# Narrow-tile matmuls of a pair of heads side by side, bank halves out of sequence, and GpSimd adds of half a tile

## The chip, the cores and the metric

The kernel runs on one core of one Trainium2 chip. The metric is the device time of one execution in microseconds. The engines of the core are TensorE (PE, with weight loads as PEld), VectorE (DVE), ScalarE (ACT), GpSimd (POOL) and SyncE (SP), which here issues nearly all DMAs. Each engine works through its own instructions in order and waits on semaphores for the others.

## The reference

Per head, attention over keys that fall in the same hash bucket; then a soft mixture of experts over all tokens.

```python
q, k, v: (4, 8, 768, 64) float32; proj: (64, 6)
q_bits, k_bits = (q @ proj > 0), (k @ proj > 0)          # 6 bits = 64 buckets
mask   = bucket(q)[:, :, :, None] == bucket(k)[:, :, None, :]
scores = where(mask, q @ k.T / 8, -1e9)
attn   = exp(scores - scores.max(-1)); attn /= attn.sum(-1) + 1e-9
x      = (attn @ v) as (3072, 512)                        # B*S tokens, H*D features
logits = x @ phi                                          # (3072, 32), 8 experts x 4 slots
d = softmax(logits, axis=0); slot_in = d.T @ x            # over tokens
slot_out[e] = relu(slot_in[e] @ w1[e]) @ w2[e]            # w1 512x1024, w2 1024x512
out = softmax(logits, axis=1) @ slot_out
```

## The kernel before

There are 32 heads (4 batches of 8), taken in pairs. A head has 768 queries and keys, as 6 blocks of 128. Per pair, `load` brings q and k, ScalarE and VectorE split them into high and low parts (`split_hi`, `split_lo`, tile w4), and SyncE moves the parts into the operand tiles XY of each head (`spread_y`, `spread_l`, `spread_x`, through `move`, L296). `bits` (L328) makes the hash bits of the pair with 32-column matmuls, and `spread_bits` moves them (tile bt) into XY. Three XY tiles go round.

Per head, `smax` (L370) multiplies for the row maxima: 12 matmuls, of 512 and 256 columns in turn, where matmuls n = 1 and 2 of every four fill two halves of one PSUM bank, behind which one VectorE reduction stands (L373; L376 for the whole banks). `shift` (L382 to L385) turns maxima into offsets, `shift_rows` (L404 transpose of 12 columns, L407 copy on ScalarE, a DMA mr into XY) puts them in a row of XY. `scores` (L421) then multiplies keys by queries, two matmuls each, in the same pattern of banks, and L425 takes the exponential into one of three tiles pt, each for two key blocks. `acc` adds the six key blocks of pt on GpSimd (L432 for the first two, L438 for the rest), 128x768 at a time. `av` (L449) multiplies by v for j = 0, 1, 2, each four matmuls with 64 columns of output on TensorE (the trace shows them as x8); v lies in one of two tiles, loaded by `load_v` (L278).

Per pair, `pair_sum` (L461) sums acc over keys with 32-column matmuls; L464 copies the sums on ScalarE, `pair_rec` takes reciprocals; `pair_log` (L476, 32 columns) makes the logits of the experts; `pair_turn` (L496) and `pair_x` (L511) transpose. After each eight heads a batch of the soft mixture is folded in (L607 to L661 and beyond); the experts' two layers and the output follow behind the last head, some 60 us. Their weights, 512 KB each, are loaded by `load_weights` (L190, L192) in between.

The order is written out by hand: `at` gives each piece a time, and a sort by it sets the order of the code. The times come from the table WHEN, in slots counted from the head's start (6 slots a head, even and odd heads apart), with overrides for the first and last heads in FIRST. Every engine's queue, SyncE's included, follows that order. SyncE's DMAs share eight semaphores in rotation.

Of the kernel before, what the change touches and what calls it, by code (L numbers as in the profile page):

```python
# [9 lines left out]
F32 = mybir.dt.float32  # L10
F32R = mybir.dt.float32r
AF = mybir.ActivationFunctionType
ALU = mybir.AluOpType
# [3 lines left out]
B, H, S, D, NB = 4, 8, 768, 64, 6  # L17
BH = B * H
P = 128
NT = S // P  # L20
HC = S // 2
# [12 lines left out]
N_Y = 3  # L34
# [7 lines left out]
C_ALL = C_FD + P  # L42


WHEN = {'load': -23.456,
 'bits': -14.465,
 'split_hi': -14.035,
 'split_lo': [-13.1, -12.626],
 'spread': [[-12.12, -11.747, -10.749, -7.5], [-12.05, -10.773, -10.639, -11.794]],
 'load_v': [-1.88, -1.85],  # L50
 'smax': [[-8.153, -7.646, -7.592, -7.407, -6.31, -6.263, -5.991, -5.086, -4.829, -4.442, -4.009, -3.019],
          [-7.926, -7.769, -7.645, -6.916, -6.247, -6.159, -6.133, -5.32, -4.829, -3.608, -3.608, -3.119]],
 'scores': [[-0.175, 0.609, 1.069, 1.557, 1.767, 2.599, 2.628, 3.37, 4.446, 4.862, 5.118, 5.577],
            [0.788, 1.398, 1.492, 1.906, 2.213, 2.62, 2.628, 3.37, 4.011, 4.193, 4.382, 4.945]],
 'shift': [-2.471, -2.398],
 'shift_rows': [-2.151, -1.917],
 'acc': [[5.646, 6.72, 8.258], [5.625, 6.02, 9.329]],
 'av': [[3.513, 6.554, 6.938], [3.513, 5.087, 6.68]],
 'pair_sum': 16.448,
 'pair_turn': 18.256,  # L60
 'pair_rec': [18.379, 18.389, 18.942],
 'pair_log': 18.557,
 'pair_x': [22.815, 24.33],
 'pair_add': 19.89,
 'batch_both': 20.1,
 'batch_max': 22.4,
 'batch_exp': 23.0,
 'batch_turn': 23.9,
 'batch_scale': 24.396,
 'batch_slots': 26.173,  # L70
 'batch_weigh': 24.65,
 'batch_share': 27.6,
 'load_weights': 4.18}

FIRST = {('load', 4): 4.476,
# [72 lines left out]
def lsh_attention_soft_moe(  # L148
# [11 lines left out]
    nc = tc.nc  # L160
# [35 lines left out]
    st = [dict() for _ in range(BH)]  # L196
# [8 lines left out]
    pts = [held.tile([P, 2 * S], F32, name=f"pt{j}") for j, held in enumerate((ap, lp, mp))]  # L205
    accs = [(mp if i == (BH - 1) % 3 else ap).tile([P, S], F32, name=f"acc{i}") for i in range(3)]
    vs = [held.tile([P, NT, D], F32, name=f"v{i}") for i, held in enumerate((ap, mp))]
# [31 lines left out]
    p_sm = ps_stack.enter_context(tc.tile_pool(name="p_sm", bufs=2, space=PSUM))  # L239
    p_st = ps_stack.enter_context(tc.tile_pool(name="p_st", bufs=3, space=PSUM))  # L240
# [13 lines left out]
    Ys, Xs = [], []  # L254
    XYs = []
    for i in range(N_Y):
        held = lp if i == (BH - 1) % N_Y else yp
        XYs.append(held.tile([P, 2, 2, S], F32R, name=f"XY{i}"))
        Xs.append(XYs[i][:, :, 0])
        Ys.append(XYs[i][:, :, 1])  # L260
    row = accs[0][0:1]
    nc.gpsimd.memset(row, 1.0)

# [10 lines left out]
    lacc_of = {}  # L274

    def load_v(h):
        st[h]["v"] = vs[h % 2]
        nc.sync.dma_start(out=st[h]["v"], in_=vt[h])  # L278


# [13 lines left out]
    def move(dst, src, eng=nc.sync):  # L294

        eng.dma_start(out=dst.bitcast(F32), in_=src.bitcast(F32))  # L296


    def spread_y(h):
        s = st[h]  # L300
        s["XY"], s["Y"] = XYs[h % N_Y], Ys[h % N_Y]
        if h == 0:
            return
        r = 64 * (h % 2)
        move(s["Y"][0:64], s["w4"][r:r + 64, 0::2])
# [6 lines left out]

    def spread_x(h):
        s = st[h]
        s["X"] = Xs[h % N_Y]
        r = 64 * (h % 2)
        move(s["X"][0:64], s["w4"][r:r + 64, 0::3])
        move(s["X"][96:128], s["w4"][r + 32:r + 64, 1:3])
# [40 lines left out]

    def smax(h, t, part):  # L360
        s = st[h]
        if t == 0 and part == 0:
            s["mx"] = mp.tile([P, NT, 2], F32, name="mx", bufs=2)
        mx = s["mx"].rearrange("p t a -> p (t a)")
        n = 2 * t + part
        if n % 4 != 2:
            s["sm_ps"] = p_sm.tile([P, 512], F32, name="smx")
        pt = s["sm_ps"]
        o, a, b = ((0, 0, 512), (0, 512, S), (256, 0, 256), (0, 256, S))[n % 4]
        nc.tensor.matmul(pt[:, o:o + b - a], s["Y"][0:96, 0, t * P:(t + 1) * P], s["Y"][0:96, 1, a:b],  # L370
                         start=True, stop=True)
        if n % 4 == 2:
            nc.vector.tensor_reduce(out=mx[:, n - 1:n + 1], in_=pt.rearrange("p (a x) -> p a x", a=2),  # L373
                                    axis=AX.X, op=ALU.max)
        elif n % 4 != 1:
            nc.vector.reduce_max(out=mx[:, n:n + 1], in_=pt, axis=AX.X)  # L376
# [34 lines left out]
    def scores(h, i, part):  # L411
        s = st[h]
        n = 2 * i + part
        if n % 4 == 0:
            s["P", i // 2] = pts[i // 2]
        if n % 4 != 2:
            s["st_ps"] = p_st.tile([P, 512], F32, name="st")
        pt = s["st_ps"]
        o, a, b = ((0, 0, 512), (0, 512, S), (256, 0, 256), (0, 256, S))[n % 4]
        for x, first in ((s["Y"], True), (s["X"], False)):  # L420
            nc.tensor.matmul(pt[:, o:o + b - a], x[:, 1, i * P:(i + 1) * P], x[:, 0, a:b],  # L421
                             start=first, stop=not first)
        if n % 4 != 1:
            u = (0, 0, 1, 2)[n % 4]
            nc.scalar.activation(s["P", i // 2][:, 512 * u:512 * u + 512], pt, AF.Exp, scale=D ** -0.5)  # L425

    def acc(h, j):
        s = st[h]
        pr = s["P", j]
        if j == 0:  # L430
            s["acc"] = accs[h % 3]
            nc.gpsimd.tensor_tensor(out=s["acc"], in0=pr[:, 0:S], in1=pr[:, S:2 * S], op=ALU.add)  # L432
        else:
            for a in range(2):
                n = 2 * j + a
                eng = nc.vector if h == BH - 1 and n > 2 else nc.gpsimd
                if h < BH - 1 or n < NT - 1:
                    eng.tensor_tensor(out=s["acc"], in0=s["acc"], in1=pr[:, a * S:(a + 1) * S], op=ALU.add)  # L438

    def av(h, j, half=None):  # L440
        s = st[h]
# [273 lines left out]
    def at(when, f, *args):  # L715
        key = (f.__name__, *(a for a in args if isinstance(a, int)))
        plan.append((FIRST.get(key, when), len(plan), (f, *args)))
# [10 lines left out]
    for h in range(BH):  # L728
        s0, x = NT * h, h % 2
        if x == 0:  # L730
            if h > 0:
                at(s0 + WHEN["load"], load, h)
            at(s0 + WHEN["bits"], bits, h)
            at(s0 + WHEN["split_hi"], split_hi, h)
            for n in range(2):
                at(s0 + WHEN["split_lo"][n], split_lo, h, n)
        for n, f in enumerate((spread_y, spread_bits, spread_l, spread_x)):
            at(s0 + WHEN["spread"][x][n], f, h)
        at(s0 + WHEN["load_v"][x], load_v, h)
        for n in range(2 * NT):  # L740
            at(s0 + WHEN["smax"][x][n], smax, h, n // 2, n % 2)
            at(s0 + WHEN["scores"][x][n], scores, h, n // 2, n % 2)
        at(s0 + WHEN["shift"][x], shift, h)
        at(s0 + WHEN["shift_rows"][x], shift_rows, h)
        for j in range(NT // 2):
            lone = h == BH - 1 and j == NT // 2 - 1
            at(s0 + (5.725 if lone else WHEN["acc"][x][j]), acc, h, j)
            if lone:
                for n in range(2):
                    at(s0 + 5.85 + n, av, h, j, n)  # L750
            else:
                at(s0 + WHEN["av"][x][j], av, h, j)
        if x and h < BH - 1:
            p, p0 = h - 1, s0 - NT
            at(p0 + WHEN["pair_sum"], pair_sum, p)
            at(p0 + WHEN["pair_turn"], pair_turn, p)
            for n in range(3):
                at(p0 + WHEN["pair_rec"][n], pair_rec, p, n)
            at(p0 + WHEN["pair_log"], pair_log, p)
            at(p0 + WHEN["pair_x"][0], pair_x, p, (0, 1))  # L760
            at(p0 + WHEN["pair_x"][1], pair_x, p, (2,))
            at(p0 + WHEN["pair_add"], pair_add, p)
        if h % H == H - 1 and h < BH - 1:
            for f in (batch_both, batch_max, batch_exp, batch_turn, batch_scale, batch_slots, batch_weigh, batch_share):
                at(p0 + WHEN[f.__name__], f, h // H)
    last, h = NT * BH, BH - 1
# [62 lines left out]
    for x in range(2):  # L829
        pt = p_mi.tile([P, 512], F32, name="mi")[:, 0:2 * P]  # L830
# [179 lines left out]
```

## Time and profile before

| | |
|---|---|
| three runs, us | 521.5, 524.3, 527.04 (median 524.3) |
| the profiled execution's own time, us | 524.46 |
| its span, us | 522.4 |
| mean granted clock of TensorE | 0.987 |
| busy: PE, DVE, ACT, POOL, us | 499.2, 369.3, 246.6, 326.8 |
| chain that ended last, by engine | PE 70%, DVE 10%, DMA and its queue 13%, POOL 2% |

A row of the timeline gives start and length in us, the engine, the line, the operation, what it writes and reads, the form, and a count where equal instructions are joined; in brackets the idle time before it and what ended it. Matmuls overlap, so the price of one is the distance from its start to the next start, not its length. A row of the groups gives total busy time and mean ns. A row of the chain is a piece of the path that ended last. A row of the windows gives busy time of the engines in one stretch, then the clock, the share of DMA time and the rate.

### The profile page before, as it was taken

Reading aid. Unit: us, or ns where it says so; the run is one execution under the profiler, and the core shown is the slowest. Engines: PE = TensorE matmul, PEld = TensorE weight load, DVE = VectorE, ACT = ScalarE, POOL = GpSimd, SP = SyncE. Lnnn points to the kernel's source line nnn. Section 1 sums busy time; section 2 is a strip of 40 time slices with the busy share of each in tenths; the row PEclk is TensorE's granted clock in tenths of the full one; section 3 lists DMA queues with packets and bytes.
Section 4 is the critical chain, followed back from the end, with each engine's and each line's share of the span. In section 5 each row is a group of like instructions: output and inputs, shape, how many; then the busy total and the mean of one; then the engine's idle time right before and its main releaser. Section 6 shows DMA issues by size and latency. Waiting matters only on the chain.

```text
span 522.4 us, 9095 instructions
## 1 busy us (share of the span) xinstructions
PE 499.2 (96%) x3164; PEld 284.3 (54%) x3164; DVE 369.3 (71%) x703; ACT 246.6 (47%) x463; POOL 326.8 (63%) x223
## 2 busy tenths in 40 slices
PE   7968999999999999999999999999999999999992
PEld 4544555555555555556554555565555555553562
DVE  6574877787878787777787788787777885464233
ACT  4144536464646454545454545454644545422232
POOL 9246767676739776767488785856588767411200
PEclk9789999999999999999999999999999999999998
DMA  5747475758585657575765757676636366879967
GB/s 126 188 98 188 116 196 173 193 168 197 169 197 168 178 143 203 152 210 143 217 149 167 183 175 178 188 181 182 146 101 154 73 156 234 319 286 352 410 275 293
DMA packets 39777, 99.59 MB, mean 191 GB/s; under 512 B 7458, under 2 KB 13732, under 8 KB 39732
## 3 DMA queue, kind: packets, MB, share of 16 engines
q1 hardware_dynamic: 39540, 98.94, 66.3%
q8 instruction: 25, 0.41, 0.3%
q14 instruction: 20, 0.16, 0.1%
q0 software_dynamic: 192, 0.08, 0.1%
HBM read 52.76 MB, written 6.29 MB: 113 GB/s over the span
## 4 chain that ended last, share of the span: by engine, by line
PE 70%; DVE 10%; SPq 7%; DMA 6%; POOL 2%; issue 2%; ACT 1%; DVEq 0%; ACTq 0%; POOLq 0%
PE st L421 20%; PE av L449 19%; PE smx L370 13%; SPq L296 7%; DMA XY<-bt 4%; PE qs L933 3%; DVE w L292 3%; PE qh L851 3%; DVE mx L376 3%; PE mi L461 2%; PE mi L476 2%; POOL acc L438 1%; PE mi L328 1%; DMA w<-w 1%; DMA XY<-w 1%
## 5 line engine op out<-in xcount | busy, mean ns | idle before, releaser
L438 POOL TENSOR_TENSOR acc<-acc,pt 128x768 f32<-128x768 f32 x125 | 238.8, 1911 | 39.4 <-ACT pt L425 27.1
L425 ACT ACTIVATE pt<-st 128x512 f32<-128x512 f32 x288 | 162.0, 595 | 97.2 <-PE st L421 90.8
L421 PE MATMUL st<-XY 128*128 128x512 f32 (+1 forms) x768 | 183.7, 347 | 0.0
L376 DVE TENSOR_REDUCE mx<-smx 128x1 f32<-128x512 f32 x192 | 130.8, 687 | 54.1 <-PE smx L370 53.8
L449 PE MATMUL av<-pt,v 128*64 128x384 f32 x768 | 145.3, 499 | 0.0
L370 PE MATMUL smx<-XY 96*128 96x512 f32 (+1 forms) x384 | 126.6, 375 | 9.9 <-DVE mx L376 5.4
L421 PEld LDWEIGHTS st<-XY 128*128 128x128 f32 x768 | 123.7, 191 | 21.1 <-issue 10.6
L370 PEld LDWEIGHTS smx<-XY 96*128 96x128 f32 x384 | 70.1, 191 | 74.4 <-DVE mx L376 26.1
L432 POOL TENSOR_TENSOR acc<-pt 128x768 f32<-128x768 f32 x32 | 58.6, 1830 | 63.8 <-ACT pt L425 63.8
L449 PEld LDWEIGHTS av<-pt,v 128*64 128x64 f32 x768 | 46.5, 136 | 62.7 <-issue 57.5
L373 DVE TENSOR_REDUCE mx<-smx 128x2 f32<-128x512 f32 x96 | 65.6, 683 | 4.3 <-PE smx L370 4.1
L292 DVE TENSOR_TENSOR w<-raw,w 128x768 fp32r<-128x768 f32 x30 | 41.2, 1373 | 3.7 <-ACT w L288 3.7
L468 DVE RECIPROCAL sm<-sm 128x128 f32<-128x128 f32 x45 | 39.6, 910 | 0.0
L288 ACT CAST w<-raw 128x768 fp32r<-128x768 f32 x32 | 25.1, 831 | 19.5 <-DMA XY<-w 9.7
L453 ACT COPY avs<-av 128x384 f32<-128x384 f32 x32 | 15.3, 478 | 37.2 <-PE av L449 37.2
L407 ACT CAST mr<-mi 12x128 fp32r<-12x128 f32 x31 | 7.9, 255 | 49.2 <-PE mi L404 44.6
L321 DVE TENSOR_SCALAR bt<-mi,con 128x384 fp32r<-128x384 f32 x15 | 10.1, 677 | 25.3 <-DMA XY<-bt 9.6
L607 POOL TENSOR_TENSOR dl<-lacc,dl 64x384 f32<-64x384 f32 x3 | 3.0, 999 | 25.6 <-ACT dl L606 25.6
L513 DVE TENSOR_TENSOR xq<-mi,r 128x256 f32<-128x256 f32 x45 | 17.3, 412 | 0.4 <-PE mi L511 0.4
L328 PE MATMUL mi<-raw,pb 128*32 128x384 f32 x128 | 15.2, 517 | 0.1
L933 PE MATMUL qs<-w 128*32 128x256 f32 x232 | 15.2, 382 | 0.0
L511 PE MATMUL mi<-ident,avs 128*128 128x128 f32 x90 | 14.8, 273 | 0.0
(173 smaller groups left out, 339.4 us busy)
## 6 DMA issues: line engine op xcount, KB each, us to landing
w<-w SPq DMA_DIRECT2D x61, 512.0 KB
XY<-w SPq DMA_DIRECT2D x63, 384.0 KB
raw<-qk SPq DMA_DIRECT2D x32, 384.0 KB
XY<-w SPq DMA_DIRECT2D x64, 192.0 KB
v<-vt SPq DMA_DIRECT2D x32, 192.0 KB
out<-w SPq DMA_DIRECT2D x12, 512.0 KB
xq<-w SPq DMA_DIRECT2D x3, 512.0 KB
XY<-bt SPq DMA_DIRECT2D x62, 19.5 KB
```

The lines of the kernel that those rows point to most:

```text
L292: (nc.vector if h else nc.gpsimd).tensor_tensor(out=w[:, 2 * x + 1], in0=st[h]["raw"][:, x], in1=w[:, 2 * x], op=ALU.subtract)
L296: eng.dma_start(out=dst.bitcast(F32), in_=src.bitcast(F32))
L370: nc.tensor.matmul(pt[:, o:o + b - a], s["Y"][0:96, 0, t * P:(t + 1) * P], s["Y"][0:96, 1, a:b], start=True, stop=True)
L373: nc.vector.tensor_reduce(out=mx[:, n - 1:n + 1], in_=pt.rearrange("p (a x) -> p a x", a=2), axis=AX.X, op=ALU.max)
L376: nc.vector.reduce_max(out=mx[:, n:n + 1], in_=pt, axis=AX.X)
L421: nc.tensor.matmul(pt[:, o:o + b - a], x[:, 1, i * P:(i + 1) * P], x[:, 0, a:b], start=first, stop=not first)
L425: nc.scalar.activation(s["P", i // 2][:, 512 * u:512 * u + 512], pt, AF.Exp, scale=D ** -0.5)
L432: nc.gpsimd.tensor_tensor(out=s["acc"], in0=pr[:, 0:S], in1=pr[:, S:2 * S], op=ALU.add)
L438: eng.tensor_tensor(out=s["acc"], in0=s["acc"], in1=pr[:, a * S:(a + 1) * S], op=ALU.add)
L449: nc.tensor.matmul(s["av"][64 * c:64 * c + 64, 0:HC], s["v"][:, i, :], pr[:, o + c * HC:o + (c + 1) * HC], start=(i == 0), stop=(i == NT - 1))
L468: nc.vector.reciprocal(out=rs[:, k * P:(k + 1) * P], in_=rs[:, k * P:(k + 1) * P])
L933: nc.tensor.matmul(po[32 * j:32 * j + 32], hTs[g][:, f, 32 * j:32 * j + 32], wt[1, x, 2 * g + f // 4, j][:, (f % 4) * HM:(f % 4 + 1) * HM] ...
```

## The change

The table of times is new in nearly all entries, and code is changed so that the new order can be built: the two halves of a bank may be issued apart, with other banks between them, and the tiles of a head are known from the start. GpSimd adds 384 columns at a time, twice as often. The last head keeps its old times for av. The numbers of instructions are else unchanged.

```diff
-WHEN = {'load': -23.456,
+WHEN = {'load': -20.249,
...
- 'load_v': [-1.88, -1.85],
+ 'load_v': [-0.013, 1.668],
...
+    for h in range(BH):
+        st[h].update(XY=XYs[h % N_Y], X=Xs[h % N_Y], Y=Ys[h % N_Y], v=vs[h % 2], acc=accs[h % 3])
+        st[h].update((("P", j), pt) for j, pt in enumerate(pts))
...
     def smax(h, t, part):
         s = st[h]
-        if t == 0 and part == 0:
+        if "mx" not in s:
             s["mx"] = mp.tile([P, NT, 2], F32, name="mx", bufs=2)
...
         if n % 4 != 2:
-            s["sm_ps"] = p_sm.tile([P, 512], F32, name="smx")
-        pt = s["sm_ps"]
+            s["sm_ps", n] = p_sm.tile([P, 512], F32, name="smx")
+        pt = s["sm_ps", n - (n % 4 == 2)]
...
     def scores(h, i, part):
...
-            s["st_ps"] = p_st.tile([P, 512], F32, name="st")
-        pt = s["st_ps"]
+            s["st_ps", n] = p_st.tile([P, 512], F32, name="st")
+        pt = s["st_ps", n - (n % 4 == 2)]
...
         if j == 0:
-            s["acc"] = accs[h % 3]
-            nc.gpsimd.tensor_tensor(out=s["acc"], in0=pr[:, 0:S], in1=pr[:, S:2 * S], op=ALU.add)
+            for c in (slice(0, HC), slice(HC, S)):
+                nc.gpsimd.tensor_tensor(out=s["acc"][:, c], in0=pr[:, 0:S][:, c], in1=pr[:, S:2 * S][:, c], op=ALU.add)
...
                 if h < BH - 1 or n < NT - 1:
-                    eng.tensor_tensor(out=s["acc"], in0=s["acc"], in1=pr[:, a * S:(a + 1) * S], op=ALU.add)
+                    for c in (slice(0, HC), slice(HC, S)):
+                        eng.tensor_tensor(out=s["acc"][:, c], in0=s["acc"][:, c], in1=pr[:, a * S:(a + 1) * S][:, c], op=ALU.add)
...
-                at(s0 + WHEN["av"][x][j], av, h, j)
+                at(s0 + (WHEN["av"][x][j] if h < BH - 1 else (3.513, 5.087)[j]), av, h, j)
```

Line numbers move up by one or two from L278 on (av is L448, the sums L460, the logits L475, the XY moves L298), v's load is L280.

The first place is TensorE in a pair of the middle of the run, around the sums. pt_81 to pt_83 are the three tiles of exponentials, v_87 and v_88 the v of the even and the odd head, XY_133 to XY_135 the operands of three heads, acc_85 and acc_86 the sums over key blocks. Before:

```order
L449 MATMUL av<-pt_81,v_87 64x384 x4
L370 MATMUL smx<-XY_135 128x512
L404 MATMUL mi<-ident,mz 12x128
L370 MATMUL smx<-XY_135 128x256 x2
L421 MATMUL st<-XY_133 128x512 x2
L461 MATMUL mi<-acc_85,ones 32x384 x2
L461 MATMUL mi<-acc_86,ones 32x384 x2
L370 MATMUL smx<-XY_135 128x512
```

and in the changed kernel:

```order
L448 MATMUL av<-pt_81,v_87 64x384 x4
L460 MATMUL mi<-acc_85,ones 32x384 x2
L460 MATMUL mi<-acc_86,ones 32x384 x2
L404 MATMUL mi<-ident,mz 12x128
L370 MATMUL smx<-XY_135 128x512
L419 MATMUL st<-XY_133 128x256 x2
```

The sums and the transpose of the odd head's offsets now follow directly on the even head's first product with v. Some rows on, on TensorE, around the logits, before:

```order
L496 MATMUL mi<-ident,sm 128x128 x3
L449 MATMUL av<-pt_82,v_87 64x384 x4
L476 MATMUL mi<-avs,phs 32x384 x4
L421 MATMUL st<-XY_134 128x512 x2
L370 MATMUL smx<-XY_135 128x512
L449 MATMUL av<-pt_83,v_87 64x384 x4
L370 MATMUL smx<-XY_135 128x512
```

and in the changed kernel:

```order
L370 MATMUL smx<-XY_135 128x512
L475 MATMUL mi<-avs,phs 32x384 x4
L448 MATMUL av<-pt_82,v_87 64x384 x4
L448 MATMUL av<-pt_83,v_87 64x384 x4
L370 MATMUL smx<-XY_135 128x512 x2
L419 MATMUL st<-XY_134 128x512 x4
```

The logits now stand ahead of the second and third product of the even head, which are side by side.

The second place is SyncE's queue of the same pair from the row move (mr) of the odd head on; w_2724 and w_2816 are the split parts (w4), w is a weight of the experts. Before:

```order
L296 DMA XY_134<-mr 1x12x128
L278 DMA v_88<-vt 128x384
L190 DMA w<-w 128x1024
L296 DMA XY_135<-w_2724 64x2x768
L296 DMA XY_135<-w_2724 32x2x768
L296 DMA XY_133<-w_2724 64x2x768 x2
L296 DMA XY_133<-w_2724 32x2x768
L296 DMA XY_133<-bt 13x384 x2
L296 DMA XY_133<-bt 12x384 x2
```

and in the changed kernel:

```order
L298 DMA XY_134<-mr 1x12x128
L190 DMA w<-w 128x1024
L298 DMA XY_135<-w_2816 64x2x768
L298 DMA XY_135<-w_2816 32x2x768 x2
L298 DMA XY_133<-w_2816 64x2x768
L298 DMA XY_133<-bt 13x384 x2
L298 DMA XY_133<-bt 12x384 x2
L280 DMA v_88<-vt 128x384
```

The load of the odd head's v went from the second place to the last, and one large move of XY_133 to behind it.

The third place is SyncE's queue at the last two heads, where the experts' weights are loaded. Before:

```order
L278 DMA v_87<-vt 128x384
L190 DMA w<-w 128x1024 x4
L296 DMA XY_134<-mr 1x12x128
L278 DMA v_88<-vt 128x384
L190 DMA w<-w 128x1024 x4
L192 DMA w<-w 128x1024 x11
```

and in the changed kernel:

```order
L280 DMA v_87<-vt 128x384
L190 DMA w<-w 128x1024 x3
L298 DMA XY_134<-mr 1x12x128
L190 DMA w<-w 128x1024 x4
L192 DMA w<-w 128x1024 x2
L280 DMA v_88<-vt 128x384
L192 DMA w<-w 128x1024 x9
```

The last head's v now stands behind six weight loads.

More of the change, by code (lines that the diff above doesn't have):

```diff
@@ L42 @@
 C_ALL = C_FD + P
-WHEN = {'load': -23.456,
[L46 to L49, printed above, removed]
- 'load_v': [-1.88, -1.85],
[L51 to L72, printed above, removed]
+WHEN = {'load': -20.249,
+ 'bits': -14.229,
+ 'split_hi': -14.469,
+ 'split_lo': [-12.593, -12.307],
+ 'spread': [[-8.873, -8.628, -4.884, -6.051], [-10.66, -10.364, -10.117, -8.499]],
+ 'load_v': [-0.013, 1.668],
+ 'smax': [[-7.891, -7.253, -6.89, -6.827, -4.575, -5.887, -4.897, -4.184, -4.405, -3.626, -3.436, -6.587],
+          [-8.119, -7.886, -7.155, -6.373, -6.078, -6.011, -4.493, -5.588, -3.625, -2.796, -2.553, -3.994]],
+ 'scores': [[-0.043, 1.163, 1.625, 2.761, 0.577, 1.651, 2.152, 4.632, 5.195, 4.559, 5.142, 4.685],
+            [-0.586, -0.207, 1.227, 2.283, 2.074, -0.029, 2.493, 3.261, 5.447, 3.307, 5.002, 5.509]],
+ 'shift': [-2.838, -2.089],
+ 'shift_rows': [-2.486, -1.921],
+ 'acc': [[3.889, 5.034, 5.737], [3.898, 5.254, 6.706]],
+ 'av': [[3.899, 7.565, 7.571], [3.365, 5.792, 6.373]],
+ 'pair_sum': 15.998,
+ 'pair_turn': 17.461,
+ 'pair_rec': [17.523, 18.844, 17.946],
+ 'pair_log': 19.428,
+ 'pair_x': [18.368, 24.222],
+ 'pair_add': 19.51,
+ 'batch_both': 19.679,
+ 'batch_max': 21.206,
+ 'batch_exp': 23.21,
+ 'batch_turn': 25.393,
+ 'batch_scale': 25.508,
+ 'batch_slots': 27.498,
+ 'batch_weigh': 27.829,
+ 'batch_share': 29.729,
  'load_weights': 4.18}
@@ L276, in load_v @@
     def load_v(h):
-        st[h]["v"] = vs[h % 2]
         nc.sync.dma_start(out=st[h]["v"], in_=vt[h])
@@ L300, in spread_y @@
         s = st[h]
-        s["XY"], s["Y"] = XYs[h % N_Y], Ys[h % N_Y]
         if h == 0:
@@ L314, in spread_x @@
         s = st[h]
-        s["X"] = Xs[h % N_Y]
         r = 64 * (h % 2)
@@ L413, in scores @@
         n = 2 * i + part
-        if n % 4 == 0:
-            s["P", i // 2] = pts[i // 2]
         if n % 4 != 2:
-            s["st_ps"] = p_st.tile([P, 512], F32, name="st")
-        pt = s["st_ps"]
+            s["st_ps", n] = p_st.tile([P, 512], F32, name="st")
+        pt = s["st_ps", n - (n % 4 == 2)]
         o, a, b = ((0, 0, 512), (0, 512, S), (256, 0, 256), (0, 256, S))[n % 4]
```

## The prediction

> **What bounds the kernel now.** I read the split of busy time first, then the chain that ended last, then the timeline of TensorE over one pair of heads, then the DMA issues of SyncE over the same pair. The first row gives stretch, its length, and the busy time of PE, PEld, DVE, ACT and POOL, the granted clock, DMA share and GB/s:
>
> ```profile
> 60.00:380.00 320.00, 317.79 (x1871) 180.60 (x1869) 251.01 (x454) 166.84 (x312) 227.16 (x127) 1.00 0.66 176
> ```
>
> TensorE is without work for 2.2 of 320 us at clock 1.00, while GpSimd has 93 us free and VectorE 69. So in the attention part the time is what TensorE's queue costs, one instruction after another. The chain gives the length of a pair. Its rows are start, length, engine and work; each av row below with 8 matmuls is the first product with v of an even head:
>
> ```profile
> 60.56 1.44 PE av L449 x8
> ...
> 223.04 1.44 PE av L449 x8
> ...
> 246.87 0.92 PE st L421 x4
> 249.21 1.44 PE av L449 x8
> ...
> 278.42 1.44 PE av L449 x8
> ...
> 357.59 1.44 PE av L449 x8
> ```
>
> From 223.04 to 249.21 a pair takes 26.17 us. From 249.21 to 278.42 it takes 29.21, because that pair holds a batch of the soft MoE (L661). The eleven pairs from 60.56 to 357.59 take 297.03; two of them hold a batch, so the other nine take (297.03 - 2 x 29.21) / 9 = 26.51. That is 0.34 above the clean 26.17: what a pair loses on average to waits. The row at 246.87 gives the plain price of a 512-column matmul: 0.92 / 4 = 0.23.
>
> Where the 26.17 holds something other than plain matmuls shows in the timeline (start, length, line, form):
>
> ```profile
> 197.54 0.50 PE L370 MATMUL smx<-XY 96*128 96x512 f32 x1
> 197.88 0.27 PE L404 MATMUL mi<-ident,mz 128*12 128x128 f32 x1
> 197.91 0.48 PE L370 MATMUL smx<-XY 96*128 96x256 f32 x2
> 198.23 0.63 PE L421 MATMUL st<-XY 128*128 128x512 f32 x2
> 198.79 0.85 PE L461 MATMUL mi<-acc,ones 128*32 128x384 f32 x8
> 199.57 0.50 PE L370 MATMUL smx<-XY 96*128 96x512 f32 x1
> 199.91 1.10 PE L421 MATMUL st<-XY 128*128 128x256 f32 x6
> ...
> 201.74 1.51 PE L449 MATMUL av<-pt,v 128*64 128x384 f32 x8
> 203.18 0.85 PE L476 MATMUL mi<-avs,phs 64*32 64x384 f32 x8
> ```
>
> and, from the last head,
>
> ```profile
> 458.05 0.87 PE L449 MATMUL av<-pt,v 128*64 128x384 f32 x4
> 458.84 0.44 PE L511 MATMUL mi<-ident,avs 128*128 128x128 f32 x2
> ```
>
> The reader is to compare starts. Two 512-column matmuls ahead of the sums take 198.79 - 198.23 = 0.56, which is 0.09 more than 2 x 0.233: the price of going into narrow tiles (64 or 32 columns). The 512-column matmul behind them takes 199.91 - 199.57 = 0.34, so 0.105 more: the price of coming back. Half an av group takes 458.84 - 458.05 = 0.79, so two halves apart would be 1.58, against 203.18 - 201.74 = 1.44 for a whole one: 0.14 is paid inside a group once per visit. A visit of av thus costs 0.09 + 0.14 + 0.105 = 0.33 beyond its work. The lone L404 pays as well: the matmul ahead of it takes 0.34, the two 256-column ones behind it 0.32 in place of 0.24.
>
> **The change part by part.** *Neighbours on TensorE.* Before, a pair visits narrow tiles at av, L404, L461, av with L476, av, av with L328 and L404, av, av. After, the order has av with sums and L404; logits and two av; av with L404 and bits; av; av. Eight visits become five. (a) The sums beside av: gone are one return behind av (0.105), the return behind the lone L404 (0.10), and the entry ahead of the sums (0.09), together 0.30. The change between 64 and 32 columns is not free: av takes 1.44 ahead of L476, as ahead of a full matmul, so I count that exit in full on both sides. (b) The logits and two av in a row: one return (0.105), one entry (0.09) and one inside price (0.14), together 0.33. (c) L404 ahead of bits in place of behind: 0. The sum is 0.63 a pair, or 15 x 0.63 = 9.5 us. (d) The batch's matmuls (L661) also stand beside av: one entry and one return, 0.2 to 0.3, in three batches: 0.7 us. The Trainium skill, page "TensorEngine Tiling (Array Packing)", Key Properties, states that changing the tiling mode, and not just the tile, drains TensorE; 1.44 ahead of L476 agrees. Taken alone the rule would count changes, 18 a pair before and 13 after, which at half a visit (0.165) each is 0.8 a pair and 12.4 us in all.
>
> *Bank halves out of sequence.* The matmuls, exponentials and maxima are as many as before, so 0 on TensorE. A bank is now held from its first half to the second, while others pass; three st banks and two smx banks bear that in the order, except that about 0.1 us of waiting for a maximum is possible at some places. Before, waits cost 0.34 a pair by the above; the bits now come earlier in front of the maxima that need them. I take those 0.34 down to 0.13, so -3 (from -5 with all gone to +3 with 0.2 more).
>
> *GpSimd by halves.* These are two rows of the groups (mean ns behind the comma), and below them three of the chain:
>
> ```profile
> L438 POOL TENSOR_TENSOR acc<-acc,pt 128x768 f32<-128x768 f32 x125 | 238.8, 1911 | 39.4 <-ACT pt L425 27.1
> L607 POOL TENSOR_TENSOR dl<-lacc,dl 64x384 f32<-64x384 f32 x3 | 3.0, 999 | 25.6 <-ACT dl L606 25.6
> ```
>
> ```profile
> 127.14 2.37 DMA XY<-bt
> 132.27 0.86 DVE w L292
> 133.74 2.42 DVE w L292
> ```
>
> A half is bounded by 1911 / 2 = 0.96 from below and by the 384-column add's 1.00, with some 0.08 between two, from above. Ten adds a pair then take 19.1 to 21.6 us in place of 19.1, in a pair of 25.5. That stays off the path: the cover is some 4 us of GpSimd's own slack, so 0. VectorE's w (L292) takes 0.86 alone and up to 2.42 when it meets GpSimd; with halves it can be held about 1.0 less at a time, which is part of the -3 above. The Trainium skill, page "SBUF — State Buffer", Who interferes with whom, states that such a VectorE instruction with two SBUF inputs contends with a GpSimd instruction that reads SBUF; 0.86 against 2.42 agrees.
>
> *v of the odd head.* In SyncE's queue this load moves from right behind the row move (mr) to behind one weight load, four moves of w and the four of bt. SyncE's rows of that burst before, the DMA of the same stretch (last two figures: share, GB/s), and the sizes of these loads:
>
> ```profile
> 225.39 0.78 SPq L296 DMA_DIRECT2D XY<-mr  x1
> 226.21 0.50 SPq L278 DMA_DIRECT2D v<-vt  x1
> 226.75 0.43 SPq L190 DMA_DIRECT2D w<-w  x1
> 227.23 6.05 SPq L296 DMA_DIRECT2D XY<-w  x5
> 233.33 4.25 SPq L296 DMA_DIRECT2D XY<-bt  x4
> ```
>
> ```profile
> 225.40:238.30 12.90, 12.90 (x84) 6.86 (x82) 10.02 (x19) 6.20 (x11) 8.48 (x6) 1.00 0.74 184
> ```
>
> ```profile
> w<-w SPq DMA_DIRECT2D x61, 512.0 KB
> XY<-w SPq DMA_DIRECT2D x63, 384.0 KB
> ...
> XY<-w SPq DMA_DIRECT2D x64, 192.0 KB
> v<-vt SPq DMA_DIRECT2D x32, 192.0 KB
> ```
>
> I add up the new order with the prices above (the clean pair of before comes to 26.15 in this way, against 26.17 measured). In pair time, 0 being the first av of the even head, L404 of the odd head then stands at 2.2, and its row move issues some 1.0 later, since the logarithm of the sums (L464 before) now goes ahead of the copy on ScalarE: 3.2. The odd head's first av stands at 14.05. Early bound: without backlog an XY move issues in about 0.7 and a bt move in 0.75, so v issues at 0.8 + 0.43 + 4 x 0.7 + 4 x 0.75 = 7.0 after mr, takes 0.5, and lands 2.4 later (the 2.37 of the bt move): 9.9, so 13.1 of the pair, 0.9 in time. Late bound: with the backlog shown, w, XY and bt took from 226.75 to 237.58 = 10.8; with one XY fewer 9.6; then 0.8 + 9.6 + 0.5 + 2.4 = 13.3, so 16.5, or 2.4 late. By bytes: 2.3 MB (0.5 of w, 1.5 of three large and two small XY moves, 0.2 of v, the rest small) went in 12.9 us at 184 GB/s; now one large XY move less, 1.9 MB, go, v last, in 10.5 plus about 1 of landing. I take the middle of the bounds, 11.6, which the bytes support: v lands at 14.8 and TensorE stands 0.75. Behind av on its queue then waits everything else, so it is paid in full. The weight load is there for 12 odd heads; the other three are 0.5 MB / 184 = 2.8 earlier and in time. So +9.0 us, from 0 to 29.
>
> *v of the last head.* It now stands behind six weight loads of 512 KB; before it was ahead of them. SyncE's rows, the DMA while the loads run, and TensorE's first av of heads 30 and 31:
>
> ```profile
> 441.32 0.69 SPq L278 DMA_DIRECT2D v<-vt  x1
> 442.58 1.75 SPq L190 DMA_DIRECT2D w<-w  x4
> ```
>
> ```profile
> 442.58:453.20 10.62, 10.62 (x63) 4.46 (x61) 4.20 (x7) 5.37 (x11) 7.78 (x5) 1.00 0.85 315
> ```
>
> ```profile
> 438.44 1.51 PE L449 MATMUL av<-pt,v 128*64 128x384 f32 x8
> ...
> 451.40 1.51 PE L449 MATMUL av<-pt,v 128*64 128x384 f32 x8
> ```
>
> Its first av ran 451.40 - 438.44 = 12.96 behind that of head 30. The loads can start once head 30's last scores are done, 5.4 behind head 30's first av in the new order; 3.3 MB at 315 GB/s take 10.6, and a landing lags about 1: 17 against 13.1. I take 3.6 (from 0, were v to overtake the loads, to 5). All that follows shifts with it.
>
> *Start and the MoE's end:* same work, 0.
>
> The sum: -9.5 - 0.7 - 3 + 9.0 + 3.6 = -0.6, and +2 for waits of the new order on maxima and row moves that I can't place (the row move lands 0.1 us ahead of its scores, bounds -1 and +5): +1.4. Against the profiled run's own 524.46 that is 526. The median of the runs is 524.3, so it stands equal.
>
> **The rivals.** A: v of odd heads is in time, since SyncE's queue is freer than in the burst shown. For it: the early bound, 0.9 to spare. Against: the bytes. Then 526 - 9 = 517, and 513 if the last v is also in time. B, the other side: the backlog holds as shown, v is 1.3 to 2.4 late, the late bound. It decides from a landing 12.2 us after mr on; the price is 12 x 1.8 = 22 in place of 9: 539. C: narrow neighbours save less than thought, as each change of columns pays what a visit paid: only two av in a row gain, 0.33 a pair, 526 + 4.5 = 530. Against it: the entry and return are seen on the full matmuls around, which are fewer. D: GpSimd's halves cost over 1.27 each, so twenty exceed the pair of 25.5; at 1.35 a pair is 27: 526 - 9 (v is then in time) + 12 x 1.5 = 535. Against it: the 1.00 of L607.
>
> **How the numbers follow.** My forecast, v late by 0.2 to 1.2 a pair, 519 to 532, gets 0.47; A 0.27; B 0.14; C 0.08; D 0.04. About 1% (519.2 to 529.7) is what a measurement can tell from no change. Faster: 0.25 of A and 0.03 of mine, 0.28. Slower: B, D, half of C and 0.11 of mine, 0.33. Within 1%: 0.39. The range 515 to 538 leaves out the fast edge of A (0.08) and the slow half of B with D's edge (0.1).
>
> **What would show it.** A pair without waits of 25.5 in the chain; sums starting 1.44 behind the even head's first av; the second of two av groups at 1.29; GpSimd's half at 0.96 to 1.04. TensorE's waits should name v's load at the odd head's first av, about 0.75 each in 12 pairs, and once 3 to 4 us at head 31. No such wait and a pair of 25.6 would prove A; waits of 2 us B; pairs of 26 without waits C. If TensorE waits chiefly for maxima or row moves, the step that put waits at -3 and +2 was wrong.

## The result and the profile after

The changed kernel takes 545.5 us (median of four runs, 541.38 to 550.04), against 523.65 for the kernel before beside it: a ratio of 1.0385, with a 95% interval of 1.0294 to 1.0475. The forecast was 526, with 515 to 538 as its range. The profiled execution of the changed kernel has a span of 543.7 us. All ratios, here and below, are taken over executions in the faster of the chip's two states and against executions of the kernel before from the same round, while the times are medians of all executions, so a difference of two times from different rounds can be off by one or two us.

The same window as before the change, the middle of the attention part (busy time of PE, PEld, DVE, ACT, POOL, clock, DMA share, GB/s):

```profile
60.00:380.00 320.00, 302.82 (x1787) 179.04 (x1787) 249.73 (x432) 154.81 (x294) 229.16 (x236) 1.00 0.64 167
```

TensorE now stands 17 of 320 us, where it stood 2; VectorE and GpSimd are about as busy as they were although fewer heads pass in the window, ScalarE is less so for that reason, and the clock is the same. So the loss is waiting. The list of TensorE's waits (us in total, times, longest) names what for:

```profile
PE av L448 <- DMA v<-vt: 15.6, 14, 1.5
PE mi L404 <- DVE mz L385: 5.2, 16, 0.6
PE smx L370 <- DVE mx L376: 4.5, 3, 3.8
PE st L419 <- ACT pt L423: 1.6, 3, 0.8
```

The third row is nearly all at the start, as before. The first is new; the second stood there once before, with 1.1 us. The list counts only idle time behind the modelled end of a matmul. A lone 512-column matmul is 0.40 long in the rows while the next one starts 0.23 behind it, so a delay of some 0.1 us shows in the starts alone. TensorE's timeline shows where in a pair the waits fall; here are the rows that matter of the pair from 230.12 to 257.76:

```profile
230.12 1.51 PE L448 MATMUL av<-pt,v 128*64 128x384 f32 x8
231.56 0.85 PE L460 MATMUL mi<-acc,ones 128*32 128x384 f32 x8
232.69 0.28 PE L404 MATMUL mi<-ident,mz 128*12 128x128 f32 x1 [0.28 <-DVE mz L385]
232.90 0.47 PE L370 MATMUL smx<-XY 96*128 96x512 f32 x1
...
238.40 0.85 PE L475 MATMUL mi<-avs,phs 64*32 64x384 f32 x8
239.18 2.80 PE L448 MATMUL av<-pt,v 128*64 128x384 f32 x16
241.91 0.73 PE L370 MATMUL smx<-XY 96*128 96x512 f32 x2
...
245.69 1.51 PE L448 MATMUL av<-pt,v 128*64 128x384 f32 x8 [0.86 <-DMA v<-vt]
247.14 0.28 PE L404 MATMUL mi<-ident,mz 128*12 128x128 f32 x1
247.34 0.85 PE L328 MATMUL mi<-raw,pb 128*32 128x384 f32 x8
...
257.76 1.51 PE L448 MATMUL av<-pt,v 128*64 128x384 f32 x8
```

The pair takes 27.64 where the order summed to 25.5. The neighbours themselves cost what was forecast: the sums follow 1.44 behind av, the logits take 0.78, and the two av in a row take 2.73 to the next start, which is 1.44 + 1.29. But L404 starts 2.57 into the pair, not 2.2; the odd head's first av starts 15.57 into it, not 14.05. I took the starts of every pair against the plain prices. Over the ten pairs without a batch that hold bits, from 59 to 430 us, the medians are: L404 0.37 late, and the next matmul 0.21 behind it where 0.03 was usual (0.55 in all); 0.17 more behind the second L404, ahead of bits; 1.2 at that av; and 0.35 in pieces, most of them of 0.07 to 0.1 and ahead of scores. With the 25.5 that makes 27.8, against a median pair of 27.9. From the first even head's first av to the last one's the changed kernel needs 423.1 us, against 404.7; the start is 0.5 shorter, and what follows 3.5 longer.

### The profile page after: what moved, and what is told of

It reads as the page before. It is cut to its first block, busy times and chain, and to the rows that moved or that the text cites. A ratio compares the mean times of both kernels' runs of the same rounds, so it can differ in the third digit from the quotient of the medians.

```text
span 543.7 us, 9273 instructions
## 1 busy us (share of the span) xinstructions
PE 501.1 (92%) x3164; PEld 293.1 (54%) x3164; DVE 384.6 (71%) x705; ACT 242.9 (45%) x463; POOL 340.1 (63%) x380
## 4 chain that ended last, share of the span: by engine, by line
PE 55%; DVE 15%; DMA 12%; SPq 12%; issue 3%; ACT 2%; DVEq 0%; ACTq 0%
PE st L419 16%; PE av L448 12%; SPq L298 11%; PE smx L370 10%; DMA v<-vt 8%; DVE mx L376 4%; DVE mx L373 4%; DVE mz L385 3%; PE qs L932 3%; PE qh L850 3%; DVE mz L383 2%; PE mi L328 2%; DMA XY<-mr 2%; PE mi L510 2%; PE mi L475 2%
## 5 line engine op out<-in xcount | busy, mean ns | idle before, releaser
L437 POOL TENSOR_TENSOR acc<-acc,pt 128x384 f32<-128x384 f32 x250 | 249.2, 1027 | 41.7 <-ACT pt L423 41.7
L419 PE MATMUL st<-XY 128*128 128x512 f32 (+1 forms) x768 | 176.2, 344 | 1.7 <-ACT pt L423 1.6
L448 PE MATMUL av<-pt,v 128*64 128x384 f32 x768 | 143.1, 500 | 16.9 <-DMA v<-vt 15.6
L376 DVE TENSOR_REDUCE mx<-smx 128x1 f32<-128x512 f32 x192 | 128.9, 685 | 35.4 <-PE smx L370 35.2
L370 PE MATMUL smx<-XY 96*128 96x512 f32 (+1 forms) x384 | 132.5, 381 | 6.1 <-DVE mx L376 4.5
L419 PEld LDWEIGHTS st<-XY 128*128 128x128 f32 x768 | 126.8, 190 | 19.5 <-ACT pt L423 5.9
L430 POOL TENSOR_TENSOR acc<-pt 128x384 f32<-128x384 f32 x64 | 62.6, 999 | 74.6 <-ACT pt L423 74.3
L448 PEld LDWEIGHTS av<-pt,v 128*64 128x64 f32 x768 | 49.4, 137 | 82.7 <-issue 64.3
L290 ACT CAST w<-raw 128x768 fp32r<-128x768 f32 x32 | 25.1, 830 | 29.9 <-DMA XY<-mr 22.4
L294 DVE TENSOR_TENSOR w<-raw,w 128x768 fp32r<-128x768 f32 x30 | 29.8, 994 | 9.9 <-ACT w L290 9.9
L385 DVE SCALAR_TENSOR_TENSOR mz<-m,mz 128x6 f32<-128x6 f32 x32 | 28.6, 893 | 1.1
L463 ACT ACTIVATE sm<-mi,eps 128x384 f32<-128x384 f32 x15 | 8.7, 581 | 24.7 <-PE mi L460 24.7
L512 DVE TENSOR_TENSOR xq<-mi,r 128x256 f32<-128x256 f32 x45 | 16.6, 395 | 0.4 <-PE mi L510 0.3
L404 PEld LDWEIGHTS mi<-ident,mz 128*12 128x12 f32 x31 | 2.6, 85 | 26.1 <-DVE mz L385 15.3
L383 DVE TENSOR_SCALAR mz<-m 128x6 f32<-128x6 f32 x32 | 15.2, 474 | 1.1
## 6 DMA issues: line engine op xcount, KB each, us to landing
XY<-bt SPq DMA_DIRECT2D x62, 19.5 KB
```

What stands on the lines that cost most here:

```text
L294: (nc.vector if h else nc.gpsimd).tensor_tensor(out=w[:, 2 * x + 1], in0=st[h]["raw"][:, x], in1=w[:, 2 * x], op=ALU.subtract)
L385: nc.vector.scalar_tensor_tensor(out=mz[:, 0:NT], in0=m, scalar=-1.0, in1=mz[:, NT:2 * NT], op0=ALU.mult, op1=ALU.subtract)
L430: nc.gpsimd.tensor_tensor(out=s["acc"][:, c], in0=pr[:, 0:S][:, c], in1=pr[:, S:2 * S][:, c], op=ALU.add)
L437: eng.tensor_tensor(out=s["acc"][:, c], in0=s["acc"][:, c], in1=pr[:, a * S:(a + 1) * S][:, c], op=ALU.add)
L448: nc.tensor.matmul(s["av"][64 * c:64 * c + 64, 0:HC], s["v"][:, i, :], pr[:, o + c * HC:o + (c + 1) * HC], start=(i == 0), stop=(i == NT - 1))
```

## The experiments

### The odd head's v back in its place

```diff
- 'load_v': [-0.013, 1.668],
+ 'load_v': [-0.013, -1.85],
```

> The changed kernel with the odd head's load of v put back right behind the row move, for all odd heads, the last one too. Theory 1 (the place in SyncE's queue is the cause): the wait for v goes from 14 pairs and from the last head, 14 to 15 times 1.37 us and 3.7 us, so 545.5 - 20 - 3.7 = about 522 us, a little under the time of before; a pair is about 26.1. Rival 2 (VectorE's offsets, L385 beside GpSimd, hold the pair, and v is merely the wait that comes last): TensorE's waits for L385 grow, the pair stays over 27, the time stays over 535. Rival 3 (the weight load and the XY moves, now behind v, become late in their turn): a wait for XY moves of over 0.5 us a pair, 530 or more.

Measured: 536.23 us, ratio to before 1.0233 (1.0167 to 1.03). All waits for v are gone, but only 9.3 us of the 20 to 24 expected. A pair without a batch still takes 27.0 to 28.3. TensorE's waits in v_early:

```profile
PE mi L404 <- DVE mz L385: 5.8, 19, 0.6
PE smx L370 <- DVE mx L376: 5.4, 4, 4.5
PE st L419 <- ACT pt L423: 4.4, 8, 1.2
```

The third row has grown from 1.6 to 4.4. The timeline of ScalarE, SyncE and TensorE in v_early tells why:

```profile
219.00 1.57 ACT L290 CAST w<-raw 128x768 fp32r<-128x768 f32 x2 [2.75 <-DMA XY<-mr]
220.48 2.09 ACT L423 ACTIVATE pt<-st 128x512 f32<-128x512 f32 x4
```

```profile
212.81 2.14 SPq L298 DMA_DIRECT2D XY<-w  x3
216.28 0.82 SPq L298 DMA_DIRECT2D XY<-mr  x1
```

```profile
221.12 0.73 PE L419 MATMUL st<-XY 128*128 128x512 f32 x2 [0.43 <-ACT pt L423]
```

The cast of the next pair (L290) writes w4, of which there is one, so it must wait for SyncE's last moves out of it, issued from 212.81 on behind the whole burst. The bracket names the row move, the last of several semaphores, which came at 218.71; by its semaphore the last move out of w4 had landed at 218.55. It stands 2.75 us on ScalarE; four exponentials queue behind it, and the first scores of the next head find no free bank. So v was the later of two things that SyncE's burst made late, and moving it uncovered the other; the next run tests that. Theory 1 holds for the place, not for the sum; rival 2 and rival 3 each had a part.

### Two buffers for w4, and the weight load out of the burst

```diff
-N_WA, N_WB, N_WY, N_WP, N_WL, N_WC = 23, 5, 6, 3, 5, 1
+N_WA, N_WB, N_WY, N_WP, N_WL, N_WC = 20, 5, 6, 3, 5, 1
...
-        w = pp.tile([P, 4, S], F32R, name="w4", bufs=1)
+        w = pp.tile([P, 4, S], F32R, name="w4", bufs=2)
```

> The changed kernel with v early for odd heads (as v_early) and two buffers in place of one for the split parts w4, for which three of the experts' weights are loaded late, at the end. Theory: in v_early ScalarE stands up to 2.8 us ahead of its cast (L290), which waits until SyncE's moves have read w4, and the exponentials behind it hold TensorE's banks, 0.4 to 0.5 us at the next head's first scores; with two buffers this goes, a pair falls from 27.2 to about 26.7, the attention part by 6 to 8 us, and the end is 0 to 4 us longer: 528 to 534 us. Rival: the wait is for the banks themselves, used out of sequence; then the pair stays at 27.2 and the time at 536 or above.

Measured: 536.62 us, 1.0204 (1.0158 to 1.025). The pairs without a batch are now 26.8 to 27.2, and the attention part from the first to the last even head fell from 416.2 to 408.6 us. The wait for the exponentials is no longer among the longest nine, and ScalarE's wait ahead of the cast, 28.8 us in 11 times in v_early, is down to 0.2. The start is 4 us shorter too. The end, however, grew by 10 us, not 0 to 4, for the three late weights. The mechanism holds; as a whole it gains nothing. So I took the load off the burst instead:

```diff
 # v_early
- 'load_weights': 4.18}
+ 'load_weights': 3.6}
```

> As v_early, with the weight load of the odd head's segment moved from right behind the row move to the light segment of the even head, ahead of the next pair's q and k; so the moves of w4 run 512 KB (some 2.7 us) earlier. Theory: in v_early the last moves of w4 hold ScalarE's cast and so TensorE's banks, and what is late is SyncE's burst; the wait at the first scores of the next even head goes (a pair 27.2 to 26.8, as two buffers of w4 gave it), with no cost at the end: 536 - 6 = about 530 us. Rival: the weight load now lands ahead of the next row move and makes that late: as slow or slower.

Measured: 532.7 us, 1.0145 (1.0046 to 1.0244); pairs of 26.8 to 27.5, the wait for the exponentials' banks 1.1. That is the burst's part. The 530 forecast was 6 below v_early; the ratios (1.0233 and 1.0145) say 4 to 5, with overlapping intervals.

### The row transposes later

```diff
 # v_early_w
- 'bits': -14.229,
+ 'bits': -14.4865,
- 'shift_rows': [-2.486, -1.921],
+ 'shift_rows': [-2.486, -1.885],
```

> As v_early_w (v early, the weight load out of the burst), with the row transposes L404 placed later on TensorE: behind the bits for the even head, and behind one more matmul for maxima for the odd head, as the kernel before has them. Theory (what is left of the changed kernel's loss is TensorE at L404, waiting for VectorE's offset L385, which GpSimd holds up, and paying a way out of 12 columns of its own): a pair falls from 26.8 to 26.3 or 26.5, the waits for L385 from 5.8 to under 2 us, the time from 532.7 to 525 to 529. Rival (the remaining 1.3 us over the clean 25.5 are banks and maxima out of sequence): the pair stays at 26.8.

Measured: 525.01 us, 0.9987 (0.9966 to 1.0008), pairs of 26.4 to 26.8 but for one of 27.2. No wait for L385 is left among the longest. In its timeline L404 has the next start 0.04 behind it (220.63 to 220.67), where it had 0.21 in the changed kernel. The rival, banks out of sequence, would have left the pair at 26.8; but the pair didn't reach the clean 25.5 either. These are rows of TensorE in the odd half of a pair, with delays that the list of waits doesn't hold:

```profile
238.45 0.50 PE L370 MATMUL smx<-XY 96*128 96x512 f32 x1
239.07 0.73 PE L419 MATMUL st<-XY 128*128 128x512 f32 x2
...
243.20 0.40 PE L370 MATMUL smx<-XY 96*128 96x512 f32 x1
243.43 0.40 PE L419 MATMUL st<-XY 128*128 128x256 f32 x2
243.67 0.50 PE L370 MATMUL smx<-XY 96*128 96x512 f32 x1
244.01 0.63 PE L419 MATMUL st<-XY 128*128 128x512 f32 x2
```

The matmul at 243.20 has its plain 0.23 to the next start. The one at 243.67 has 0.34 with no narrow tile beside it, and the one at 238.45, behind an av, has 0.62 in place of 0.34. By their semaphores, the scores behind both wait until ScalarE's exponential has freed a bank. In this run such delays sum to 0.7 to 1.4 a pair, and without them nine of the ten pairs come to 25.64 to 25.71. The largest, mostly 0.2 to 0.5, stands where ScalarE's cast for the next pair is still 0.7 to 1.7 late; in v_early_w4, where the cast waits for nothing, that one is gone and two or three of 0.07 to 0.1 are left at the same places of each pair.

Why L385 is late is seen in the groups (mean ns behind the comma). The changed kernel, v_early_whole (below), and the kernel before:

```profile
L385 DVE SCALAR_TENSOR_TENSOR mz<-m,mz 128x6 f32<-128x6 f32 x32 | 28.6, 893 | 1.1
L383 DVE TENSOR_SCALAR mz<-m 128x6 f32<-128x6 f32 x32 | 15.2, 474 | 1.1
```

```profile
L383 DVE TENSOR_SCALAR mz<-m 128x6 f32<-128x6 f32 x32 | 36.8, 1152 | 1.1
L385 DVE SCALAR_TENSOR_TENSOR mz<-m,mz 128x6 f32<-128x6 f32 x32 | 10.0, 313 | 1.1
```

```profile
L383 DVE TENSOR_SCALAR mz<-m 128x6 f32<-128x6 f32 x32 | 10.8, 336 | 1.1
L385 DVE SCALAR_TENSOR_TENSOR mz<-m,mz 128x6 f32<-128x6 f32 x32 | 6.0, 188 | 1.1
```

Two instructions of six columns take 0.5 us together before and 1.4 after. The timeline of the changed kernel, VectorE and GpSimd:

```profile
231.15 0.53 DVE L383 TENSOR_SCALAR mz<-m 128x6 f32<-128x6 f32 x1
231.71 0.92 DVE L385 SCALAR_TENSOR_TENSOR mz<-m,mz 128x6 f32<-128x6 f32 x1
```

```profile
230.65 1.96 POOL L430 TENSOR_TENSOR acc<-pt 128x384 f32<-128x384 f32 x2 [1.30 <-ACT pt L423]
```

GpSimd's two halves end at 232.61, and L385 at 232.63. L383 seems to end with the first half and L385 with the second: each is held by one. Of the 32 of each line in the changed kernel, 31 end within 0.06 us of the end of a GpSimd instruction. With whole adds L383 is held for the rest of one add, and L385 runs behind it in 29 of 32 cases.

### The halves by themselves

v_early_whole is v_early with the slices of 384 columns replaced by the whole tile; before_halves and logits_w_halves are the kernel before and logits_w (below) with the halves of the change.

> As v_early, with GpSimd's adds whole (768 columns) as before the change. If the halves shorten the time for which VectorE's two-input instructions (L385 and L294) are held, as theory 1 has it, L385 is held up to 1.8 us in place of 0.9, TensorE waits for it some 0.5 to 1 us more a pair, and the time is 6 to 15 us over v_early. Rival: the halves' added starts only cost, and whole adds are as fast or 1 to 3 us faster.

> The kernel before with GpSimd's adds in halves and nothing else. Theory: GpSimd is off the path and the halves alone change the time by less than 1%: 520 to 526 us, with the mean of L292 down from 1.37 to about 1.0 us. Rival: over 529.

> logits_w, the fastest so far, with GpSimd's adds in halves. Theory: VectorE is held for less time, the waits for maxima (4.9 us in logits_w) shrink: 0 to 3 us faster, 515 to 518. Rival: the halves meet VectorE's offsets more often and cost 1 to 5 us.

Measured: v_early_whole 538.76 us, 1.0284 (1.0215 to 1.0354), 2.5 above v_early from the same round, less than the 6 to 15 expected; the intervals of the ratios overlap, though each of its four times is above each of v_early's. Its waits for L385 are 11.0 us in 30 times against 5.8 in 19. before_halves 528.4 us, 1.0056 (1.0032 to 1.008), within the 1% but above the 520 to 526. logits_w_halves 520.54 us, 0.9885 (0.986 to 0.991), 2.7 above logits_w (0.9855, 0.9773 to 0.9937), which is not told apart from it, and not the 515 to 518 expected. So by themselves the halves cost the kernel before half a per cent, and in the new order they help by some 2.5 us. In before_halves L292 falls from 1.37 to 1.17, about half as far as forecast, and L385 rises from 0.19 to 0.78. So the halves do lengthen L385, but in the new order TensorE waits longer for it without them: what costs is L404's place right behind the sums.

### The last head's v alone

```diff
+ ('load_v', 31): 184.15,
```

> The changed kernel with the load of v put back for the last head alone. Theory 1: the attention part stays as it is, the last head's first av comes at 13.0 behind that of the head before, in place of 16.6, and the time falls by 3 to 4 us, to about 542. Rival: the experts' weights, now later by one small load, or the rest of the end set the time, and the gain is under 1 us.

Measured: 543.3 us, 1.0359 (1.0279 to 1.044), 2.2 less than the changed kernel, which the intervals don't separate. The last head's first av comes 15.2 behind that of head 30, not 13.0: the waits for L385 and for exponentials are in front of it here too. In the changed kernel it came at 16.6, and the wait named v was 1.04 of that.

### The late v in the kernel before

```diff
- 'load_v': [-1.88, -1.85],
+ 'load_v': [-1.88, 1.24],
...
+ ('load_v', 31): 184.15,
```

> The kernel before with nothing changed but the odd heads' load of v, which goes behind the moves of bt as in the changed kernel (the last head's stays). Theory 1: v has 2.3 MB ahead of it there, lands about 14 us behind the row move, some 16.4 to 16.7 of the pair, and is needed at 13.45: 2.5 to 3 us a pair in those pairs with a weight load, 1 in the others, so 524 + 30 to 42 = 554 to 566 us. Rival (the neighbours and the halves are what costs, the late v is hidden by slack): under 530.

Measured: 597.94 us, 1.1308 (1.1149 to 1.1467), over the 554 to 566 expected; the profiled execution took 588.32, which is 64 above that of the kernel before. TensorE waits for v 47.1 us in 15 times. That is 3.1 a pair, just over what was expected. The rest is the clock, 0.945 in the mean against 0.987. These are a window ahead of the end of such a wait, a window around it, and TensorE's rows there:

```profile
243.00:269.50 26.50, 24.21 (x143) 14.57 (x139) 21.17 (x37) 13.69 (x25) 16.97 (x9) 1.00 0.64 172
269.90:273.10 3.20, 2.88 (x12) 0.89 (x16) 0.00 (x0) 0.00 (x0) 1.85 (x2) 0.50 0.14 39
```

```profile
270.22 2.83 PE L450 MATMUL av<-pt,v 128*64 128x384 f32 x8 [3.01 <-DMA v<-vt]
272.98 0.93 PE L329 MATMUL mi<-raw,pb 128*32 128x384 f32 x8
```

The granted clock is halved for 3.4 us around the end of 13 of these waits, and av takes 2.76 to the next start in place of 1.44. Some 1.3 us 13 times is 17 us, which with the 47 makes the 64. In the changed kernel, with waits for v of up to 1.5 us, the clock stays at 1.00 in the attention part. The place in the queue by itself is enough to lose more than the change did.

### The neighbours by themselves

```diff
 # logits_beside: the kernel before with
- 'av': [[3.513, 6.554, 6.938], [3.513, 5.087, 6.68]],
+ 'av': [[3.513, 6.936, 6.938], [3.513, 5.087, 6.68]],
- 'pair_log': 18.557,
+ 'pair_log': 18.935,
 # both_beside: also
- 'pair_sum': 16.448,
+ 'pair_sum': 15.5135,
 # both_halves: both_beside with the halves
```

> The kernel before, with two times of the table changed so that the logits and the even head's second and third product with v stand in a row on TensorE; all else as before. If the price of a visit to narrow tiles is what the prediction took from the trace, a pair falls by 0.33 us (clean pair 25.84 in place of 26.17) and the time by 5 us, to about 519. Rival (the visit's price is hidden or is paid at every change of columns): under 1 us.

> As logits_beside, and the sums put right behind the even head's first product with v (the row transpose L404 stays by itself, 0.8 us later in the pair). One return and one entry less, 0.20 us a pair: clean pair 25.64, 8 us under before in all, about 516 us. Rival: the later L404 and ScalarE's copy of the sums, now ahead of the copy of the row, make the odd head's scores wait, and the 3 us are given back.

> As both_beside, with GpSimd's adds in halves of 384 columns. The theory that the halves shorten the time for which VectorE is held: waits of TensorE for maxima and offsets shrink, 0 to 3 us under both_beside. Rival: the halves are busy more of the time and meet VectorE's offsets more often, as slow or up to 5 us slower.

Measured: logits_beside 523.22 us, 0.9941 (0.9902 to 0.998); both_beside 535.17, 1.0194 (1.0136 to 1.0252); both_halves 533.49, 1.0141 (1.0072 to 1.0209), 1.7 under both_beside and not told apart from it. The logits' gain is there, though the time fell by 3 us and not 5: from the even head's first av to the odd head's is 13.12 in nearly every pair, against 13.45 before, which is the 0.33. The sums lose 12 us. Their waits in both_beside:

```profile
PE smx L370 <- DMA XY<-bt: 8.5, 11, 1.3
PE smx L370 <- DVE mx L376: 6.0, 6, 3.4
PE smx L370 <- DMA XY<-mr: 5.6, 3, 2.2
```

The first and the third are moves on SyncE. The sums in front set L404, the row move and all that is queued behind it later, and the last of that burst are the bits that the next maxima need. The next three runs take the weight load out of that burst, in the kernel before (w_behind), in logits_beside (logits_w) and in both_beside (both_w):

```diff
- 'load_weights': 4.18}
+ 'load_weights': 7.4}
```

> The kernel before with its weight loads moved behind the moves of bits and w4 of the same segment, nothing else. Theory (SyncE's burst is nearly a bound already before): the waits for XY<-bt go, a pair comes near its clean 26.17, and the time falls by 2 to 4 us, to about 521. Rival (the burst has slack): no change.

> logits_beside with its weight loads behind the moves, as in w_behind. The 0.33 us a pair of the logits and the burst's 2 to 4 us add up: 523.2 - 3 to 5 = 518 to 520 us. Rival: the clean pair is already reached and nothing is gained over logits_beside.

> both_beside with its weight loads behind the moves. Theory (the sums beside av set the row move 0.8 us later, and with it SyncE's whole burst, whose moves of bits then come late for the next maxima): with 512 KB less in the burst the bits land 2.7 us earlier, the waits for XY<-bt and XY<-mr (15 us in both_beside) go, and the time falls from 535 to 516 to 519 us. Rival (the wait is not the burst's): it stays over 530.

Measured: w_behind 522.04 us, 0.9934 (0.9899 to 0.9969); logits_w 517.83, 0.9855 (0.9773 to 0.9937); both_w 522.59, 0.9934 (0.9903 to 0.9966). The burst was near a bound before the change, and in both_beside it was the bound: 12.6 us come back. logits_w is faster than both kernels. But both_w is no faster than w_behind and misses its 516 to 519, though its order saves 0.53 a pair by the prices; its even half takes 13.15 in most pairs where they give 12.92. The list of waits names none there, but the starts show it; TensorE, and below it VectorE:

```profile
223.03 0.63 PE L421 MATMUL st<-XY 128*128 128x512 f32 x2
223.63 0.50 PE L370 MATMUL smx<-XY 96*128 96x512 f32 x1
223.96 1.11 PE L421 MATMUL st<-XY 128*128 128x256 f32 x6
```

```profile
222.88 0.69 DVE L376 TENSOR_REDUCE mx<-smx 128x1 f32<-128x512 f32 x1 [1.73 <-PE smx L370]
```

Two 512-column matmuls take 0.60 to the next start where 0.47 is plain, and the one behind them 0.33 where 0.23 is. The one at 223.63 needs a bank that the maximum L376 frees at 223.57. The sums used to stand in between; with them gone the matmuls for maxima come too close for their two banks. These 0.13 and 0.10 are in every pair, and they are the 0.23 between 12.92 and 13.15: the sums' 0.20 is gained and lost again right behind. Without such delays seven of ten pairs come to 25.62 to 25.64, and the prices give 25.64.

## Why the prediction was wrong

**The price of a visit to narrow tiles, and the clean pair of 25.5**, were right. The logits save the 0.33 in logits_beside, and the changed kernel's av, sums and logits have the starts that the order gave. Without the delays of TensorE, both_w comes to its 25.64, and rows_behind to some 25.65 where the prices give 25.6 (25.5 and one more return, behind the lone L404). So the 9.5 us are there, and waits ate them.

**L404 ahead of bits, 0**, was too little. In the changed kernel the next start is 0.20 behind it (247.14 to 247.34); in the order of before it is 0.03. That is 0.17 a pair.

**v, +9.0 for the odd heads and +3.6 for the last.** Place and mechanism were right; the sizes were not. SyncE's rows in the pair shown:

```profile
233.32 0.75 SPq L298 DMA_DIRECT2D XY<-mr  x1
234.12 0.50 SPq L190 DMA_DIRECT2D w<-w  x1
234.67 4.66 SPq L298 DMA_DIRECT2D XY<-w  x4
239.37 3.81 SPq L298 DMA_DIRECT2D XY<-bt  x4
243.23 0.51 SPq L280 DMA_DIRECT2D v<-vt  x1
```

v issues 9.9 behind the row move, and av starts 12.4 behind it, not 11.6. Over the twelve pairs with a weight load it is 12.1 to 13.2, 12.8 in the median, so by the prediction's own mark of 12.2 rival B had the landing right. "About 1 of landing" in the sum by bytes was read off no row; here av starts 1.95 behind the end of v's issue. The wait is still 1.2 a pair and not B's 1.8, because av itself was due later by what L404 had lost. The waits named v sum to 14.6 in 13 pairs (one of them without a weight load, which was forecast to be in time) and 1.04 at the last head, 15.6 in place of 12.6. Taking v out of the place gave 9.3 of that, since ScalarE's cast behind w4's moves, at the end of the same burst, was late too, and the forecast had not followed those moves. With the weight load out of the burst as well it is 12.8. The first av of the last head came 3.7 later, as forecast, but v held it for 1.04 only and the other waits for the rest: that agreement is luck.

**GpSimd by halves, 0, and the waits of before taken from -5 to -3.** This step failed most. It asked whether GpSimd has slack and whether L292 is held, and left out L383 and L385, two small instructions which TensorE's L404 waits for. They took 0.84 us longer, L404 had been moved to right behind the sums, and a pair lost 0.55 there, some 8 us in 15 pairs. The other waits were to fall from 0.34 to 0.13 a pair and stayed at 0.35, some 3 us more, now as delays of 0.1 for the banks of the scores. The forecast had -3 for old waits and +2 for new ones, "that I can't place"; the place was L404. Setting L404 back gave 7.7, the 0.17 ahead of bits included. The last paragraph of the prediction said that this step would be wrong if TensorE waited chiefly for maxima or row moves; it waited for v and for offsets.

**The sum.** Against the forecast, v cost 5.6 more in the pairs, L404 8 and its place ahead of bits 2.6, the other waits 3, less the 2 that were allowed: some 17 of the 19.5 by which the forecast was too low. These are estimates from the medians of ten pairs, times 15. "Three st banks and two smx banks bear that in the order" does not hold to 0.1: in the new order two or three scores a pair wait for a bank. Whether the halves out of sequence or the closer order of the scores do that was tested by no run and stays open.

In ratios to before: 1.0385 as changed, 1.0233 with v early, 1.0145 with the weight load out of the burst, 0.9987 with the row transposes later.

## What to carry to other kernels

Where a queue issues one burst a period and the last of it is needed soon after, count what every moved load and every later start does to the end of the burst, and look for a second consumer that is only a little less late: taking the first wait away shows it. A dense engine gains from a better order only if the short chains that feed it have slack at the new places; list for every moved instruction what releases it, down to the ones of a quarter of a microsecond. When a price that was right brings no gain, compare the starts pair by pair: delays of 0.1 us at fixed places are in no list of waits.

## What the runs showed of the hardware that was not expected

VectorE instructions on 128x6 elements, of 0.17 us by themselves, took up to 0.93 beside GpSimd's adds of 384 columns and ended with them. With adds of half the length the hold was not halved but spread over two instructions: L383 and L385 together took 1.47 us with whole adds (v_early_whole) and 1.37 with halves (the changed kernel). The Trainium skill, page "SBUF — State Buffer", Who interferes with whom, has both cases, an instruction with two SBUF inputs and `tensor_scalar` in its two-port form; the rows agree with it for instructions as small as these.

Idle time of TensorE cost more than itself where it was long: around the end of waits of some 3 us in before_v_late the granted clock was 0.50 for 3.4 us, and av took 2.76 us in place of 1.44.
